# Half slabs, layer norm sums on ScalarE and an earlier first shift at the head of a gated long-convolution kernel

## The chip, the cores and the metric

The kernel runs on one core of a Trainium2 chip. The metric is the device time of one execution in microseconds (us); lower is better. The core's engines run side by side, each through its own list of instructions in order: TensorE (PE: matrix products and transposes, results in PSUM), VectorE (DVE), ScalarE (ACT), GpSimd (POOL) and SyncE (SP). SP, ACT and POOL also start DMAs. In the profile's rows L213 is line 213 of the kernel.

## What is computed

The forward pass normalises x, convolves a shifted and gated signal with a filter as long as the sequence, multiplies it by the output of a gated linear unit (silu on top), and adds x. The kernel returns this output and all gradients for a given grad_out.

```python
def forward(x, k, v, shift_k, ssm_k, ssm_D, w_gate, w_up, w_down):
    xn = (x - mean(x)) / sqrt(var(x) + 1e-5)           # over D = 1024
    k_shift = sum(k_pad[:, t:t + S] * shift_k[:, 3 - t] for t in range(4))
    kv = k_shift * v
    y = causal_conv(kv, ssm_k) + kv * ssm_D            # by rfft over 2 S
    s = xn * y
    h = (xn @ w_gate) * (xn @ w_up)                    # F = 3584
    return x + s * silu(h @ w_down)

out, vjp = jax.vjp(forward, ...)
return out, *vjp(grad_out)          # S = 2048, D = 1024, bfloat16
```

## The kernel before

S = 2048 rows are 16 row blocks of 128, F = 3584 columns are 14 slabs of 256 (`NSL`). The stages follow one another on TensorE, and the work of other engines is threaded between: first the gated unit's two input products, with the convolution's forward transform beside them (to about 546 us), then the down product, the backward products and the weight gradients.

**The head.** x comes in six chunks, `chunks = [(0, 1), (1, 1), (2, 2), (4, 4), (8, 4), (12, 4)]` (first block, number of blocks). SP loads them in program order between the weight slabs: x of chunks 0 and 1, slab 0 (up, then gate, 512 KB each), chunk 2, slab 1, chunks 3 to 5 (lines 866 to 872). `layer_norm` (line 554) does a chunk: for each block two `bn_stats` and a `bn_aggr` on VectorE give mean and variance, then a few small operations on all blocks of the chunk at once, with one square root on ScalarE (`root`), give 1/std (`RSTD`), and one `tensor_scalar` a block normalises it in place. TensorE turns each block, eight 128x128 transposes, and ScalarE copies it to `XNT`; the normalised rows are stored to `XNd` on POOL's queue. From block 8 on the turning is put off (`turn_rows`) and done by `turn_late` after the first group of the next unit.

**Units.** `gu_unit(sl, b0, n, w, tick)` (line 629) multiplies n blocks by one slab: n groups of eight products of 128x512 into one PSUM buffer `psg` (two of them), each emptied by a ScalarE cast into `gut`, which is stored to `GUd` on ACT's queue. VectorE multiplies the two halves to `hN`; POOL stores it to `Hd`, TensorE turns it five groups later, ScalarE copies it to `hT`, SP stores that to `HTd`. In the loop from line 881 the units of slabs 0 and 1 alternate with the layer norms; each layer norm is kept behind the last normalisation of the chunk before.

**The transform.** `conv_forward` (line 685) is a generator that yields the cost of each piece; `pump` runs it up to a fraction of the total, and `tick`, called once a group, sets that fraction: it grows in equal steps over `NT` ticks. The units in the loop have no tick (`nop`). The generator's first two steps load k and v (`load_kv`, on POOL's queue: four DMAs for k, four for v, 512-byte rows). Then come a filter load, `shift(0)` (four products with the taps `Wbc`, three sums, one product with v: eight VectorE operations on 128x4096), two turns of the filter, and eight rounds of Fourier transforms: TensorE products into `psF`, ScalarE copies to `SP`, long chains of VectorE sums `W`, `KX`, `HX`, and products back into `psY`. They need the sine tables `TF`: `mask_angles` on VectorE and `build_tables` on ScalarE (six functions and one table load), after the last layer norm.

**Order.** The program is traced in order and a scheduler orders each engine's list, earlier traced first among what is ready in its own model of time; this order is fixed before the kernel runs. `tc.issue_after(ins)` keeps the instructions of a block behind `ins` on the same engine, `keep_in_program_order` (`PIN`) keeps VectorE's transform in the traced order.

The lines in the head that set the order around the change, shortened:

```python
    if i == 3:                                  # line 894
        with tc.issue_after(xsts[4].ins):       # behind the store of chunk 4
            for _ in range(2):
                next(conv)                      # loads of k and v
    ...
    for i_, sl in ([(0, 0)], [(1, 0), (0, 1), (1, 1)], [(2, 0), (2, 1)],
                   [(3, 0), (3, 1)], [(4, 0)], [(5, 0)])[i]:
        gu_unit(sl, *xs[i_][0:2], slabs[sl], nop)
    ...
pump((SHIFT_W + 3.95) / F_TOTAL)                # line 925: shift(0)
for i_ in (4, 5):
    gu_unit(1, *xs[i_][0:2], slabs[1], tick)
```

Of the kernel before, what the change touches and what calls it, by code (L numbers as in the profile page):

```python
# [10 lines left out]
ACT = mybir.ActivationFunctionType  # L11
# [8 lines left out]
def build_kernel(  # L20
# [191 lines left out]
    def tt(o, a, b, op):  # L212
        pinned(V.tensor_tensor(o, a, b, op))  # L213
# [321 lines left out]

    def load_slab(sl, eng):
        w = fw.tile([P, DC, 2, SLW], BF16, name="wslab")
        fs = slice(sl * SLW, (sl + 1) * SLW)
        for a, wsrc in ((0, B_w_up), (1, B_w_gate)):
            last = eng.dma_start(out=w[:, :, a, :], in_=wsrc[:, fs].rearrange("(dc p) f -> p dc f", p=P))  # L540
        return w, last
# [9 lines left out]
    tr_ln, act_copy = [None], [None]  # L551
    turn_rows = []

    def layer_norm(b0, n, x4):
        def small(name, dt=F32):
            return lns.tile([P, 4], dt, name=name)[:, 0:n]
        mv = lns.tile([P, 4, 2], F32, name="mv")[:, 0:n, :]
        for i in range(n):
            bst = lns.tile([P, 2, 6], F32, name="bst")
            for hh in range(2):  # L560
                V.bn_stats(out=bst[:, hh, :], in_=x4[:, i, hh * 512:(hh + 1) * 512])
            V.bn_aggr(out=mv[:, i, :], in_=bst[:])
        var_b = small("var_b", BF16)
        V.tensor_copy(var_b, mv[:, :, 1])
        vpe = small("vpe", BF16)
# [11 lines left out]
        for i in range(n):  # L577
# [18 lines left out]
            for dc in range(DC):  # L596
                tr_ln[0] = nc.tensor.transpose(ps[:, dc, :], x4[:, i, dc * P:(dc + 1) * P], ident[:])
            act_copy[0] = nc.scalar.copy(out=XNT[q][:, :, qi * P:(qi + 1) * P], in_=ps[:])
        c, r0 = divmod(b0, 8)
        return last, root, st(xnn[:, c, r0:r0 + n, :], x4[:, 0:n, :])  # L600
# [84 lines left out]
    def conv_forward():  # L685
# [12 lines left out]
        def load_h(ds):  # L698
            hrow = U[5][:, 0:2048].rearrange("p (c u r) -> p c u r", c=2, r=8)
            cld(U[5][:, 0:2048], A_ssm_k[ds * P:(ds + 1) * P, :])  # L700
            S_["h", ds] = hrow

        def shift(dp):
# [9 lines left out]
            for j in (2, 1, 0):  # L713
                tt(prod, k[:, :, 3 - j:11 - j, :], wb(j), MUL)
                yield 2.3
                tt(acc, acc, prod, ADD)
                yield 2.3
# [42 lines left out]
        cf = pool("cf", 1)  # L760
        with tc.issue_after(xsts[3].ins):
            load_h(0)

# [89 lines left out]
        for _ in tl:  # L853
# [11 lines left out]
          for (b0, n) in chunks]  # L865
    for c in xs[0:2]:
        ln_load(*c)
    slabs = [load_slab(0, nc.sync)[0]]
    ln_load(*xs[2])
# [11 lines left out]
    for i, (b0, n, x4) in enumerate(xs):  # L881
# [9 lines left out]
        if i == 2:  # L891
            with tc.issue_after(xsts[-1].ins):
                spread_taps()
        if i == 3:
            with tc.issue_after(xsts[4].ins):
                for _ in range(2):
                    next(conv)
        if i == 4:
            with tc.issue_after(act_copy[0].ins):
                nc.scalar.activation(Dz[0:1, :], Dz[0:1, :], ACT.Copy, scale=WSC)  # L900
        for i_, sl in ([(0, 0)], [(1, 0), (0, 1), (1, 1)], [(2, 0), (2, 1)], [(3, 0), (3, 1)], [(4, 0)], [(5, 0)])[i]:
            gu_unit(sl, *xs[i_][0:2], slabs[sl], nop)
        if i == len(xs) - 1:
            with tc.issue_after(root.ins), tc.issue_after(last.ins):
                mask_angles(ang)
                build_tables(tg, ang)
    chunk[0] = len(xs)
    st(RSd.rearrange("(c u r) -> u c r", c=2, u=P), RSTD[:].rearrange("u (c r) -> u c r", c=2))
    st(RSTN[:], RSd.rearrange("(b p) -> p b", p=P))
    for p_ in (lnp, lns, tg, bsb):  # L910
        p_.release()
    ps_st.release()
    ps_cv = pool("ps_cv", 2, space=PSUM)
    pump, drain = make_pump(conv, F_TOTAL)
    cnt = [-5]
    NT = 24 * 8.0 + 17

# [6 lines left out]

    pump((SHIFT_W + 3.95) / F_TOTAL)
    for i_ in (4, 5):
        gu_unit(1, *xs[i_][0:2], slabs[1], tick)
# [708 lines left out]
```

## Time and profile before

| | us |
|---|---|
| time, median of 3 runs | 1929.6 (1929.02 to 1932.13) |
| the profiled execution, its own time | 1929.84 |
| its span, first to last instruction | 1928.1 |

| stretch, us | PE busy | DVE busy | ACT busy | POOL busy | DMA share |
|---|---|---|---|---|---|
| 0 to 10 | 7.06 | 6.98 | 2.96 | 6.04 | 0.80 |
| 10 to 20 | 8.82 | 7.70 | 4.43 | 3.34 | 1.07 |
| 20 to 50 | 27.71 | 27.48 | 20.72 | 17.03 | 0.86 |
| 50 to 73 | 23.00 | 20.12 | 19.98 | 5.00 | 0.90 |
| 73 to 367 | 293.47 | 290.79 | 170.26 | 54.73 | 0.71 |
| 367 to 488 | 118.02 | 119.86 | 67.28 | 14.34 | 0.73 |

The span is what lies between the first and the last instruction; the time of the execution holds 1.7 us more. Busy time is what an engine's instructions cover; starting a DMA is not counted. Where a row of the profile ends in square brackets, the engine stood idle for that long before it, and the name behind the arrow is what ended the wait. A line such as L213 is a helper (`tt`), so the tile names tell which step it is.

### The profile page before, as it was taken

The numbers are of one execution on the slowest core, as the hardware profiler recorded it, in microseconds if no ns is written. First come the engines' busy times: TensorE is split into PE (matmuls) and PEld (weight loads), VectorE is DVE, ScalarE is ACT, GpSimd is POOL, SyncE is SP. The second block draws the span as 40 slices with busy tenths as digits, with TensorE's granted clock in tenths as the row PEclk, the third lists the DMA queues.
The fourth block names the chain that finished last, engine by engine and source line by source line (L and its number), as shares of the span: only waits on it lengthen the run. The fifth ranks groups of instructions, "written<-read, shape, count | busy, mean of one in ns | idle before, by whom it ended". The sixth has DMA issues, their size and how long they took to land.

```text
span 1928.1 us, 27453 instructions
## 1 busy us (share of the span) xinstructions
PE 1914.2 (99%) x10978; PEld 1030.8 (53%) x10978; DVE 1542.1 (80%) x1695; ACT 638.8 (33%) x943; POOL 329.1 (17%) x461
## 2 busy tenths in 40 slices
PE   8999999999999999999999999999999999999999
PEld 5555655555444456665666666664444444444444
DVE  8999999999956555888799999999996403388884
ACT  5754655555332233343222222222222102011113
POOL 5121212201112210000122132021211101111111
PEclk9999999999999999999999999999999999999999
DMA  8776867659799988666788798585787999889984
GB/s 292 269 259 217 261 208 236 219 209 293 242 294 293 302 284 262 208 202 215 253 249 262 245 244 264 200 273 177 223 254 175 152 199 201 177 174 200 187 189 159
DMA packets 451360, 444.43 MB, mean 231 GB/s; under 512 B 268800, under 2 KB 371612, under 8 KB 436768
## 3 DMA queue, kind: packets, MB, share of 16 engines
q1 hardware_dynamic: 394848, 243.36, 47.7%
q0 software_dynamic: 40064, 169.95, 28.0%
q10 hardware_dynamic: 16320, 29.36, 4.1%
q8 instruction: 86, 1.41, 0.3%
q14 instruction: 42, 0.34, 0.1%
HBM read 194.00 MB, written 185.64 MB: 197 GB/s over the span
## 4 chain that ended last, share of the span: by engine, by line
PE 91%; DVE 6%; issue 1%; ACT 1%; DMA 0%; SPq 0%; ACTq 0%; DVEq 0%
PE psb L1344 20%; PE psx L1474 20%; PE psg L645 14%; PE psb L1327 10%; PE psbm L971 10%; PE psb L1422 9%; PE psF L235 3%; DVE W L213 2%; DVE HX L213 1%; PE tr L674 1%; PE psY L438 1%; DVE KX L213 1%; PE psY L1130 1%; PE psx L1422 1%; DVE U L213 1%
## 5 line engine op out<-in xcount | busy, mean ns | idle before, releaser
L645 PE MATMUL psg<-wslab,U 128*128 128x512 bf16 x1792 | 408.9, 380 | 3.4 <-DMA wslab<-in_B_w_gate_dram 2.5
L1344 PE MATMUL psb<-U,U 128*128 128x512 bf16 x1792 | 397.1, 379 | 0.0
L1474 PE MATMUL psx<-U,dgut 128*128 128x512 bf16 x1536 | 332.8, 379 | 0.0
L1474 PEld LDWEIGHTS <-dgut 128*128 128x128 bf16 x1792 | 175.1, 98 | 211.6
L1344 PEld LDWEIGHTS <-U 128*128 128x128 bf16 x1792 | 175.1, 98 | 198.1
L645 PEld LDWEIGHTS <-U 128*128 128x128 bf16 x1792 | 172.6, 98 | 189.0 <-issue 3.9
L1327 PE MATMUL psb<-wdt,U 128*128 128x256 bf16 x1792 | 205.6, 273 | 0.0
L1327 PEld LDWEIGHTS <-U 128*128 128x128 bf16 x1792 | 175.1, 98 | 29.4
L1422 PE MATMUL psb<-U,U 128*128 128x512 bf16 x816 | 177.1, 379 | 0.0
L213 DVE TENSOR_TENSOR W<-W 128x1024 f32<-128x1024 f32 (+1 forms) x174 | 171.5, 1002 | 3.7
L1349 ACT CAST wb<-psb 128x512 bf16<-128x512 f32 x112 | 65.6, 586 | 315.1 <-PE psb L1344 310.5
L971 PE MATMUL psbm<-U,ht 128*128 128x512 bf16 x672 | 145.7, 379 | 0.0
L1422 PEld LDWEIGHTS <-U 128*128 128x128 bf16 x896 | 87.4, 98 | 104.6
L647 ACT CAST gut<-psg 128x512 bf16<-128x512 f32 x156 | 91.4, 587 | 123.8 <-PE psg L645 123.4
L1506 ACT ACTIVATE dx_t<-dxn 128x1024 bf16<-128x1024 f32 x15 | 15.9, 1057 | 324.4 <-DVE dxn L213 324.4
L1182 DVE SCALAR_TENSOR_TENSOR dkp<-dkT,kT 128x1024 bf16<-128x1024 bf16 (+2 forms) x64 | 78.3, 1224 | 36.9 <-DMA dkT<-DKSHd 34.9
L971 PEld LDWEIGHTS <-ht 128*128 128x128 bf16 x672 | 65.5, 98 | 78.7
L213 DVE TENSOR_TENSOR U<-U,dht 128x2048 bf16<-128x2048 bf16 x56 | 68.3, 1220 | 45.7 <-ACT dht L1329 45.6
L1329 ACT CAST dht<-psb 128x512 bf16<-128x512 f32 x112 | 65.6, 587 | 116.4 <-PE psb L1327 116.4
L66 POOL DMA_DIRECT2D Hd<-hN x54 | 37.2, 688 | 296.3 <-DVE hN L213 294.1
L213 DVE TENSOR_TENSOR dxn<-psx,dxna_t 128x1024 f32<-128x1024 f32 x15 | 18.3, 1222 | 80.0 <-PE psx L1474 76.1
L1453 ACT CAST wbs<-psb 128x512 bf16<-128x512 f32 x51 | 29.9, 586 | 145.3 <-PE psb L1422 137.2
(237 smaller groups left out, 2451.5 us busy)
## 6 DMA issues: line engine op xcount, KB each, us to landing
U<-GUd SPq DMA_DIRECT2D x28, 1024.0 KB, 7.3
DGd<-U SPq DMA_DIRECT2D x28, 1024.0 KB, 6.4
GUd<-gut ACTq DMA_DIRECT2D x39, 512.0 KB, 6.1
out_dram<-wb SPq DMA_DIRECT2D x112, 128.0 KB, 4.3
U<-Hd SPq DMA_DIRECT2D x14, 1024.0 KB, 6.1
Hd<-hN POOLq DMA_DIRECT2D x54, 256.0 KB, 4.5
HTd<-hT SPq DMA_DIRECT2D x52, 256.0 KB, 3.7
ht<-HTd SPq DMA_DIRECT2D x6, 1536.0 KB, 9.7
```

Of the source, the lines that this page charges most:

```text
L213: pinned(V.tensor_tensor(o, a, b, op))
L235: mm = nc.tensor.matmul(ps[:, k].rearrange("p (c d) -> p c d", c=2), T[:, r, k, :], xr[:, r], start=(n == 0), stop=(n == len(rs) - 1 and ( ...
L645: gu_mm[0] = nc.tensor.matmul(ps[:], XNT[q][:, dc, qi * P:(qi + 1) * P], w[:, dc].rearrange("p a f -> p (a f)"), start=(dc == 0), stop=(dc ...
L647: nc.scalar.copy(out=gut[:, :, i], in_=ps[:].rearrange("p (a f) -> p a f", a=2))
L971: mm = nc.tensor.matmul(ps[:, dh * 512:(dh + 1) * 512], ht(fc)[:, i * P:(i + 1) * P], WD[fc // 4][:, fc % 4, dh * 512:(dh + 1) * 512], sta ...
L1182: ins = V.scalar_tensor_tensor(prod[:].rearrange("p r d -> p (r d)")[:, lo:H], dkT[:, 0, lo:H], 1.0, kT[:, 0, 13 + m + lo:13 + m + H], op0 ...
L1327: nc.tensor.matmul(ps[:, x * SLW:(x + 1) * SLW], DBMT[2 * hf + g][:, dc, (b % 4) * P:(b % 4 + 1) * P], wdt[:, dc, :], start=(dc == 0), sto ...
L1329: nc.scalar.copy(out=dht[:, 2 * e:2 * e + 2].rearrange("p b f -> p (b f)"), in_=ps[:])
L1344: nc.tensor.matmul(ps[:], XN[b // 4][:, b % 4, dc * P:(dc + 1) * P], dgus[b // 8][:, :, b % 8], start=(b == 0), stop=(b == NB - 1))
L1349: nc.scalar.copy(out=wb[:, dc % 2].rearrange("p a f -> p (a f)"), in_=ps[:])
L1422: nc.tensor.matmul(ps, h[:, f, b, :], DBM[b // 4][:, b % 4, dh * 512:(dh + 1) * 512], start=(b == 0), stop=(b == NB - 1))
L1474: nc.tensor.matmul(ps[:, dh * 512:(dh + 1) * 512], t[n][:, f, i * P:(i + 1) * P], WGU[n][:, f, dh * 512:(dh + 1) * 512], start=(n == 0 and ...
```

## The change

Five edits, all in the head.

- `load_slab` can load half of a slab (512 of the 1024 rows, up and gate, 256 KB each). Slab 0 is loaded in two halves, with chunk 1 of x between them, so that SP starts two DMAs more.
- In the chunks at blocks 4, 8 and 12 the last block's mean and variance are computed on ScalarE: the sum of the row by `Identity` with an accumulator, two small scalings, the sum of squared differences by `Square` with bias -mean, one small scaling. The first of these is kept behind an earlier ScalarE instruction (`hold`). `bn_stats` and `bn_aggr` remain for the other three blocks.
- The loads of k and v are traced one chunk earlier, behind the store of the chunk at block 4 and the broadcast of the taps; the first filter load has no hold any more.
- All products of `shift(0)` with the taps, and not only the first, are kept behind the last layer norm's last operation.
- The unit of slab 0 on blocks 12 to 15 moves out of the loop, behind the tables and behind the pump that traces `shift(0)`, and gets the tick; `NT` grows by 4.

```diff
@@ -533,9 +533,15 @@
     lns = pool("lns", 2)
     lnp = pool("lnp", 1)
 
-    def load_slab(sl, eng):
-        w = fw.tile([P, DC, 2, SLW], BF16, name="wslab")
+    def load_slab(sl, eng, part=None, w=None):
+        if w is None:
+            w = fw.tile([P, DC, 2, SLW], BF16, name="wslab")
         fs = slice(sl * SLW, (sl + 1) * SLW)
+        if part is not None:
+            cs_, rs_ = slice(4 * part, 4 * part + 4), slice(512 * part, 512 * part + 512)
+            for a, wsrc in ((0, B_w_up), (1, B_w_gate)):
+                last = eng.dma_start(out=w[:, cs_, a, :], in_=wsrc[rs_, fs].rearrange("(dc p) f -> p dc f", p=P))
+            return w, last
         for a, wsrc in ((0, B_w_up), (1, B_w_gate)):
             last = eng.dma_start(out=w[:, :, a, :], in_=wsrc[:, fs].rearrange("(dc p) f -> p dc f", p=P))
         return w, last
@@ -550,18 +556,30 @@
 
     tr_ln, act_copy = [None], [None]
     turn_rows = []
+    roots, copies = {}, {}
 
     def layer_norm(b0, n, x4):
         def small(name, dt=F32):
             return lns.tile([P, 4], dt, name=name)[:, 0:n]
         mv = lns.tile([P, 4, 2], F32, name="mv")[:, 0:n, :]
-        for i in range(n):
+        var_b = small("var_b", BF16)
+        own_ = n - {4: 1, 8: 1, 12: 1}.get(b0, 0)
+        hold = {4: act_copy[0], 8: roots.get(4), 12: copies.get(4)}.get(b0)
+        for i in range(own_, n):
+            junk = lnp.tile([P, D], BF16, name="junk")
+            s1, s2, negm = [lns.tile([P, 1], F32, name=nm_) for nm_ in ("s1", "s2", "negm")]
+            with tc.issue_after(hold.ins):
+                nc.scalar.activation(junk[:], x4[:, i, :], ACT.Identity, accum_out=s1[:])
+            nc.scalar.activation(negm[:], s1[:], ACT.Copy, scale=-1.0 / D)
+            nc.scalar.activation(mv[:, i, 0:1], s1[:], ACT.Copy, scale=1.0 / D)
+            nc.scalar.activation(junk[:], x4[:, i, :], ACT.Square, bias=negm[:], accum_out=s2[:])
+            nc.scalar.activation(var_b[:, i:i + 1], s2[:], ACT.Copy, scale=1.0 / D)
+        for i in range(own_):
             bst = lns.tile([P, 2, 6], F32, name="bst")
             for hh in range(2):
                 V.bn_stats(out=bst[:, hh, :], in_=x4[:, i, hh * 512:(hh + 1) * 512])
             V.bn_aggr(out=mv[:, i, :], in_=bst[:])
-        var_b = small("var_b", BF16)
-        V.tensor_copy(var_b, mv[:, :, 1])
+        V.tensor_copy(var_b[:, 0:own_], mv[:, 0:own_, 1])
         vpe = small("vpe", BF16)
         V.tensor_scalar(vpe, var_b, EPS, None, op0=ADD)
         half_r = small("half_r")
@@ -596,6 +614,7 @@
             for dc in range(DC):
                 tr_ln[0] = nc.tensor.transpose(ps[:, dc, :], x4[:, i, dc * P:(dc + 1) * P], ident[:])
             act_copy[0] = nc.scalar.copy(out=XNT[q][:, :, qi * P:(qi + 1) * P], in_=ps[:])
+        roots[b0], copies[b0] = root, act_copy[0]
         c, r0 = divmod(b0, 8)
         return last, root, st(xnn[:, c, r0:r0 + n, :], x4[:, 0:n, :])
 
@@ -711,7 +730,8 @@
                 tt(acc, k[:, :, 0:8, :], wb(3), MUL)
             yield 2.3
             for j in (2, 1, 0):
-                tt(prod, k[:, :, 3 - j:11 - j, :], wb(j), MUL)
+                with tc.issue_after(last.ins) if dp == 0 else nullcontext():
+                    tt(prod, k[:, :, 3 - j:11 - j, :], wb(j), MUL)
                 yield 2.3
                 tt(acc, acc, prod, ADD)
                 yield 2.3
@@ -758,8 +778,7 @@
         cx = pool("cx", 1)
         cs = pool("cs", 1)
         cf = pool("cf", 1)
-        with tc.issue_after(xsts[3].ins):
-            load_h(0)
+        load_h(0)
 
         def half(ds, x, i, first=None):
             if (ds, int(first is not None)) not in EIGHT:
@@ -863,9 +882,10 @@
     chunks = [(0, 1), (1, 1), (2, 2), (4, 4), (8, 4), (12, 4)]
     xs = [(b0, n, u8((4, 6, 7)[b0 // 4 - 1], a=4) if n == 4 else lnp.tile([P, n, D], BF16, name=f"x{b0}")[:])
           for (b0, n) in chunks]
-    for c in xs[0:2]:
-        ln_load(*c)
-    slabs = [load_slab(0, nc.sync)[0]]
+    ln_load(*xs[0])
+    slabs = [load_slab(0, nc.sync, 0)[0]]
+    ln_load(*xs[1])
+    load_slab(0, nc.sync, 1, slabs[0])
     ln_load(*xs[2])
     slabs.append(load_slab(1, nc.sync)[0])
     for c in xs[3:]:
@@ -891,29 +911,27 @@
         if i == 2:
             with tc.issue_after(xsts[-1].ins):
                 spread_taps()
-        if i == 3:
-            with tc.issue_after(xsts[4].ins):
                 for _ in range(2):
                     next(conv)
         if i == 4:
             with tc.issue_after(act_copy[0].ins):
                 nc.scalar.activation(Dz[0:1, :], Dz[0:1, :], ACT.Copy, scale=WSC)
-        for i_, sl in ([(0, 0)], [(1, 0), (0, 1), (1, 1)], [(2, 0), (2, 1)], [(3, 0), (3, 1)], [(4, 0)], [(5, 0)])[i]:
+        for i_, sl in ([(0, 0)], [(1, 0), (0, 1), (1, 1)], [(2, 0), (2, 1)], [(3, 0), (3, 1)], [(4, 0)], [])[i]:
             gu_unit(sl, *xs[i_][0:2], slabs[sl], nop)
-        if i == len(xs) - 1:
-            with tc.issue_after(root.ins), tc.issue_after(last.ins):
-                mask_angles(ang)
-                build_tables(tg, ang)
+    with tc.issue_after(root.ins), tc.issue_after(last.ins):
+        mask_angles(ang)
+        build_tables(tg, ang)
     chunk[0] = len(xs)
     st(RSd.rearrange("(c u r) -> u c r", c=2, u=P), RSTD[:].rearrange("u (c r) -> u c r", c=2))
     st(RSTN[:], RSd.rearrange("(b p) -> p b", p=P))
     for p_ in (lnp, lns, tg, bsb):
         p_.release()
+    turn_late()
     ps_st.release()
     ps_cv = pool("ps_cv", 2, space=PSUM)
     pump, drain = make_pump(conv, F_TOTAL)
     cnt = [-5]
-    NT = 24 * 8.0 + 17
+    NT = 24 * 8.0 + 21
 
     def tick(by=1):
         cnt[0] += by
@@ -923,6 +941,7 @@
             pump((SHIFT_W + (F_TOTAL - SHIFT_W) * (cnt[0] + 6.5) / (NT + 3.5)) / F_TOTAL)
 
     pump((SHIFT_W + 3.95) / F_TOTAL)
+    gu_unit(0, *xs[5][0:2], slabs[0], tick)
     for i_ in (4, 5):
         gu_unit(1, *xs[i_][0:2], slabs[1], tick)
     for sl in range(2, NSL - 2):
```

## The prediction

> **What bounds the kernel now.** I began with the page: TensorE is busy 1914.2 of 1928.1 us, so all that TensorE can ever get back is 13.9 us.
>
> ```profile
> PE 1914.2 (99%) x10978; PEld 1030.8 (53%) x10978; DVE 1542.1 (80%) x1695; ACT 638.8 (33%) x943; POOL 329.1 (17%) x461
> ...
> DVE  8999999999956555888799999999996403388884
> ACT  5754655555332233343222222222222102011113
> PEclk9999999999999999999999999999999999999999
> ```
>
> The second and third rows show where other engines come near their limit: VectorE (DVE) is at 9 tenths in slices 2 to 10 (48 to 482 us), and ScalarE (ACT) is at 7 in the slice from 48 us. The granted clock is full throughout, so it plays no part.
>
> Next, the waits of TensorE, longest first:
>
> ```profile
> PE tr L674 <- DVE hN L213: 3.0, 1, 3.0
> PE psg L645 <- DMA wslab<-in_B_w_gate_dram: 2.5, 2, 1.5
> PE tr L521 <- POOL ident masks.py:199: 1.4, 1, 1.4
> PE tr L597 <- DVE U L580: 1.0, 1, 1.0
> PE tr L606 <- DVE U L580: 0.7, 1, 0.7
> PE psg L645 <- ACT gut L647: 0.6, 1, 0.6
> PE psg L645 <- ACT U L587: 0.2, 1, 0.2
> ```
>
> They add up to 9.4 us (the rest is the store at the end, 3.6 us after the last matmul, and scraps). The change can reach all but the 1.4 us on `ident`. The timeline of TensorE places the ones that decide:
>
> ```profile
> 15.31 2.10 PE L645 MATMUL psg<-wslab,U 128*128 128x512 bf16 x9 [0.95 <-DMA wslab<-in_B_w_gate_dram]
> ...
> 26.30 1.99 PE L597 MATMUL tr<-ident,U 128*128 128x128 bf16 x32 [0.98 <-DVE U L580]
> ...
> 35.67 1.99 PE L606 MATMUL tr<-ident,U 128*128 128x128 bf16 x32 [0.72 <-DVE U L580]
> ...
> 40.63 3.61 PE L645 MATMUL psg<-wslab,U 128*128 128x512 bf16 x16 [0.59 <-ACT gut L647]
> ...
> 488.20 1.04 PE L674 MATMUL tr<-ident,hN 128*128 128x128 bf16 x8 [2.96 <-DVE hN L213]
> ```
>
> The last is the largest, and far from the edit. The chain of waits shows VectorE pieces without a break of TensorE from 368 to 488 us, ending in this `hN`. In the windows VectorE is busy 290.8 of 294 us (73 to 367) and 119.9 of 121 us (367 to 488): it runs behind TensorE's order the whole way, and at 488 the lag has eaten the buffers. What starts that run is in VectorE's timeline:
>
> ```profile
> 51.30 2.29 DVE L213 TENSOR_TENSOR U<-k,Wbc 128x4096 bf16<-128x4096 bf16 x1 [0.49 <-DMA k<-in_A_k_dram]
> ...
> 72.92 4.63 DVE L213 TENSOR_TENSOR W<-SP 128x1024 f32<-128x1024 f32 x4 [2.10 <-ACT SP L295]
> ```
>
> **The change, part by part.**
>
> *Slab halves: 0.* TensorE's first product now waits for the whole gate half of slab 0 (1.52 us, until 9.89). With halves, four of its eight matmuls can run earlier, but behind units (0,0) and (1,0) stands slab 1, which ends the wait at 15.31 (landed at 15.18). The bytes ahead of slab 1 are the same, and SP's issue of x2 already blocks for 2.45 us, which hides two more issues of 0.43 us. So what TensorE gains at 9.89 it waits at 15.31. x1 now stands behind 512 KB; at 261 to 332 GB/s (the page of this stretch) that is 1.5 to 2.0 us, from a landing at 5.2 (issue 1.66 plus 3.5) to about 7.0, against 6.89 at which VectorE asks for it; x2's 0.78 us of wait hides the 0.1. Bounds: -0.9 (all of the 0.95) to +0.5 (slab 1 later by an issue).
>
> *Three rows to ScalarE.* On VectorE a row costs two statistics and an aggregate, 1.15 + 0.11 = 1.26 us on the chain; three rows free 3.8 us. On ScalarE a row is five activations and two accumulator reads. `Square` and these forms are not in the trace; nearest are the sums of the last layer norm:
>
> ```profile
> 1708.41 1.06 ACT L1506 ACTIVATE dx_t<-dxn 128x1024 bf16<-128x1024 f32 x1 [63.60 <-DVE dxn L213]
> 1709.37 0.19 ACT L1506 ACTIVATION_READ_ACCUMULATOR dx_t<-dxn 128x1 f32 x1
> 1709.73 1.06 ACT L1508 ACTIVATE dx_t<-prod 128x1024 bf16<-128x1024 f32 x1 [0.17 <-DVE prod L213]
> ```
>
> Sum with read 1.15, gap 0.17, two small ones of 0.20 (the row of `half_r`), gap 0.17, square with read 1.15 (1.33 if the bias costs as in L1511, 1.24 us), gap 0.17, one of 0.20: 3.4; without gaps 2.9; I take 3.3, so 9.9 us for three, against ScalarE's idle 9.3 us in 20 to 50 us and 3.0 us in 50 to 73. That is tight, and it is the change's price.
>
> The Trainium skill, "ScalarE: Activation LUTs", section "Rules for kernel authors", says to put add- and multiply-like work on VectorE, faster per element there. The rows agree per row (1.26 against 3.3) and the rule speaks against the edit; by it alone the sum would be 6 us worse for three rows, but it counts neither engine's idle time.
>
> Chunk 4: its row may start when the copy before ends (20.34) and is done at 23.6, while VectorE ends its three rows at 18.91 + 3.78 = 22.7. Now the variance is complete at 24.24, so the chain gains 0.6 (0.98 if the row starts with no gaps; -0.4 if two casts of 0.59 go between). Value 0.6 of the 0.98 at 26.30. Chunk 8: VectorE saves 1.26 plus the 0.6 before; the 0.72 at 35.67 is gone (0 to 0.72). The 0.59 at 40.63 is four row copies of 0.94 in front of a cast; they come earlier, I take half, 0.3 (0 to 0.59).
>
> New stalls: with two accumulator buffers and 1.73 us per group, a cast of 0.59 may be 1.14 late. The longest piece on ScalarE, 1.06 + 0.19, is over that by 0.11; six such pieces, two hits: -0.2. Behind them on ScalarE stand casts, turned copies and GUd issues; TensorE waits for the casts. If a row runs unbroken it costs 3.3 + 0.59 - 1.73 = 2.2 of TensorE instead (first bound 0).
>
> *k's shift ahead of the last paceless unit.* Its loads move on POOL's queue from 37.80 to right behind the broadcast taps: four k issues (3.3 us) and four v issues (3.0 us) now stand ahead of two stores of normalised rows and several Hd stores, which nobody reads for hundreds of us; the Dz tile and `A_ssm_k` (no hold now; 4.4 us to land, needed at 64) lose nothing. k took 9 to 11 us to land, so it is there by about 42. VectorE's layer norms end at 46.5 - 3.8 = 42.7, masks 2.5 more: 45.2. Then the 1.09 and 0.49 us of gap before 51.30 go as well, and the shift ends some 5.4 us earlier (3.8 + 1.6), with part of the 2.10 at 72.92 as reserve if ScalarE has the six table functions (1.15 each) done; they are now emitted before the last unit's casts. The unit made paced puts the transform four groups (4 x 1.73 = 6.9 us) earlier in TensorE's order. NT grows by four, so at 488 the fraction of transform emitted is larger by about 0.0026 (187.5/216.5 against 183.5/212.5), 1.2 us of VectorE. Net lead there 4.2 to 6.3.
>
> To clear the stall VectorE must lead by 2.96 plus what TensorE gains before, 0.6 + 0.72 + 0.3 - 0.2 = 1.4: 4.4 in all, inside that lead. So 2.96 is taken whole (0 if the lead is under 1.4). What is late next: at 497 VectorE waits 3.34 for a cast, so the lag does not return; from there TensorE is never stopped till the end, and what is gained stays.
>
> **Sum** against the profiled execution (1929.84: span 1928.1 and 1.7 around it; the median 1929.6 is 0.24 lower, too little to matter): 1929.84 - 0.6 - 0.72 - 0.3 + 0.2 - 2.96 = 1925.5.
>
> **Rivals.**
> *A. ScalarE gives back what VectorE lends* (28%): casts are late by some 2 us in all between 20 and 60, the early waits stay in another name, only the lag wait goes: 1929.84 - 2.96 + 0.6 = 1927.5. For it: 9.9 us into 12.3 idle. Against: idle comes in pieces of 0.4 to 1.3 between casts, just where a piece fits.
> *B. ScalarE becomes the bound* (20%): at 20 to 36 us each row runs unbroken ahead of the casts, since it is emitted ahead of them, 3 x 2.2 = 6.6, and three of the tables in a row, 3.5 + 0.59 - 1.73 = 2.3; less 4.7 gained: 1929.84 + 8.9 - 4.7 = 1934.0. It decides once the casts are late by over 4.7 in all. That `Square` may not stand beside `Sqrt` in one table is the same rival: each of six reloads costs the 1.28 us of the page's table load, 7.7. Against: both tuned stretches have dependency gaps in which a cast can slip.
> *C. Slab 1 comes earlier too* (8%): the 0.95 at 15.31 and part of 1.0 at 26 and 40: 1925.5 - 0.95 - 0.6 = 1923.9. Against: same bytes, same queue.
> *D. The slab halves do nothing* is part of the forecast.
>
> **How the numbers follow.** The forecast has 44%, its own range 1924.5 to 1926.5 from the bounds above. About 0.2% (3.9 us) is what a measurement can tell from no change: 1925.7. Of the 44, 7 lie above it. Faster: 37 + 8 = 0.45; same: 7 + 28 = 0.35; slower 0.20. Range 1923.6 (C) to 1931.5: it holds the forecast, A and C and half the way to B.
>
> **What would show it.** Right: no wait of TensorE on `hN` near 480; layer norm of the last chunk done by 43; `U<-k,Wbc` starting near 45; first `W<-SP` at 66 to 69; the slab wait still ending near 15.2. Wrong: `psg <- ACT` in TensorE's waits above 1 us; a third table load before 50; VectorE waiting for `var_b` parts; the transform still starting near 72, which would leave the 2.96.

## The result and the profile after

The changed kernel takes **1932.39 us** (median of 20 runs, 1930.9 to 1936.66). In the same runs the kernel before took 1929.06 us (median of 20, 1927.31 to 1939.28). The ratio is 1.0016, with a 95% interval of 1.0009 to 1.0024, so the change costs some 3.3 us. The forecast was 1925.5 us, faster, and its range ended at 1931.5: the time is outside it, on the other side.

The profiled execution of the changed kernel took 1934.55 us, with a span of 1932.7 us (before: 1929.84 and 1928.1). From its page, busy times and the rows of 40 slices:

```profile
PE 1909.6 (99%) x10844; PEld 1033.1 (53%) x10978; DVE 1538.5 (80%) x1686; ACT 646.3 (33%) x964; POOL 329.9 (17%) x461
...
DVE  6999999999946555888799999999996403388884
ACT  6855555555522224333222222221222102011113
PEclk9999999999999999999999999999999999999999
```

TensorE's busy time looks smaller than before, but 134 of its 10978 matmul records are missing here, as the two counts beside PE and PEld show; it can't be compared. The row of ScalarE (ACT) shows 8 instead of 7 in the slice from 48 us: the engine that got the work is fuller exactly where it already stood highest. What can be compared are TensorE's waits. The list of what TensorE waited for, in us in total, times, longest:

```profile
PE psg L664 <- DMA wslab<-in_B_w_gate_dram: 3.0, 1, 3.0
PE tr L751 <- ACT hx L754: 1.6, 1, 1.6
...
PE psg L664 <- ACT gut_s L666: 1.3, 1, 1.3
PE psF L235 <- ACT hx L754: 1.3, 1, 1.3
PE psg L664 <- ACT U L666: 0.8, 1, 0.8
...
PE tr L693 <- DVE hN L213: 0.4, 1, 0.4
```

The wait on `hN` has fallen from 3.0 to 0.4 us, and the two on normalised rows, 1.0 and 0.7 us, are gone but for 0.2 (one of 0.6 us has come at the first chunks). In their place stand 3.0 us for the gate part of slab 1 (before: 1.52 us for slab 0 and 0.95 for slab 1, the 2.5 in two pieces of the list), and four entries on ScalarE of 0.8 to 1.6 us, where the kernel before has only 0.6 and 0.2. All listed waits add up to 11.7 us, against 9.4 before. The timeline of TensorE shows where they are:

```profile
16.91 4.00 PE L664 MATMUL psg<-wslab,U 128*128 128x512 bf16 x9 [3.04 <-DMA wslab<-in_B_w_gate_dram]
20.70 1.91 PE L615 MATMUL tr<-ident,x 128*128 128x128 bf16 x16
...
67.94 0.22 PE L751 MATMUL tr<-ident,U 128*128 128x128 bf16 x1 [1.64 <-ACT hx L754]
...
69.89 0.27 PE L235 MATMUL psF<-hx,TF 128*128 128x256 bf16 x1 [1.30 <-ACT hx L754]
...
494.18 0.62 PE L693 MATMUL tr<-ident,hN 128*128 128x128 bf16 x8 [0.43 <-DVE hN L213]
```

The nine products behind the slab take 4.00 us; before, the same nine took 2.10 us. The waits are not the whole price, and the windows of the same execution say why (columns: us, busy us and count of PE, PEld, DVE, ACT and POOL, then TensorE's granted clock, DMA share, GB/s):

```profile
12.00:15.00 3.00, 1.86 (x8) 0.66 (x8) 2.22 (x9) 1.58 (x4) 0.00 (x0) 1.00 1.08 398
15.00:18.00 3.00, 1.09 (x3) 0.44 (x4) 1.73 (x6) 0.00 (x0) 1.28 (x2) 0.68 1.04 422
18.00:21.00 3.00, 3.00 (x10) 1.21 (x9) 0.00 (x0) 0.48 (x1) 3.00 (x4) 0.50 1.01 413
21.00:24.00 3.00, 2.95 (x22) 2.14 (x21) 2.86 (x7) 2.03 (x3) 2.43 (x4) 0.68 1.00 407
...
68.00:72.00 4.00, 2.70 (x26) 2.35 (x26) 3.97 (x2) 4.00 (x6) 0.57 (x1) 0.84 0.42 117
72.00:76.00 4.00, 3.78 (x20) 2.28 (x20) 3.97 (x4) 2.78 (x4) 0.74 (x2) 0.74 0.56 231
```

The granted clock falls to 0.50 behind the slab wait and to 0.74 behind the waits near 68. In the profiled execution of the kernel before it is 1.00 in all these windows, and falls only once until the last product, from 488 to 492 us, behind the wait on `hN`:

```profile
488.00:492.00 4.00, 3.80 (x17) 1.98 (x18) 3.96 (x6) 1.50 (x2) 1.23 (x2) 0.57 1.07 413
```

So three things are to be told apart: the slab that lands later, the work that ScalarE can't take in time, and the clock. My theory after this reading was that each of the first two costs a part, since each has its own wait. The rivals: that one of them alone makes the whole loss; that the clock behind the slab wait does it; and that the gain at 488 never was worth what the forecast took.

### The profile page after: what moved, and what is told of

Its sections match the earlier page's. It is cut to its first block, busy times and chain, and to the rows that moved or that the text cites. A ratio compares the mean times of both kernels' runs of the same rounds, so it can differ in the third digit from the quotient of the medians.

```text
span 1932.7 us, 27330 instructions
## 1 busy us (share of the span) xinstructions
PE 1909.6 (99%) x10844; PEld 1033.1 (53%) x10978; DVE 1538.5 (80%) x1686; ACT 646.3 (33%) x964; POOL 329.9 (17%) x461
## 4 chain that ended last, share of the span: by engine, by line
PE 95%; ACT 2%; DVE 1%; issue 1%; DMA 1%; SPq 0%; ACTq 0%
PE psb L1363 20%; PE psx L1493 20%; PE psg L664 18%; PE psb L1346 10%; PE psbm L990 10%; PE psb L1441 9%; PE psF L235 3%; PE tr L693 1%; PE psY L438 1%; PE psY L449 1%; PE psY L1149 1%; PE psx L1441 1%; DMA wslab<-in_B_w_gate_dram 1%; DVE W L213 0%; PE tr L753 0%
## 5 line engine op out<-in xcount | busy, mean ns | idle before, releaser
L664 PE MATMUL psg<-wslab,U 128*128 128x512 bf16 x1734 | 403.8, 381 | 8.5 <-DMA wslab<-in_B_w_gate_dram 3.0
```

The lines of the kernel that those rows point to most:

```text
L664: gu_mm[0] = nc.tensor.matmul(ps[:], XNT[q][:, dc, qi * P:(qi + 1) * P], w[:, dc].rearrange("p a f -> p (a f)"), start=(dc == 0), stop=(dc ...
```

## The experiments

Each kernel below was timed against the kernel before on one chip (10 to 12 runs, the changed kernel 20; before's median was 1929.06 in the run of the result, 1929.14 in the series of e1, e4, e5 and e6, 1929.09 in that of e7, e8, e10 and e11, and 1929.52 in that of e3, e12 and e13). Much of the spread within a kernel goes with TensorE's clock: the shortest run of each has a mean granted clock of 1.000, and those at 0.998 are some 1.5 to 8 us longer (not all: two of the changed kernel's, 1933.13 and 1936.14 us, have 1.000). Of each kernel one execution was profiled.

| kernel | median us | lowest to highest | ratio to before, 95% interval |
|---|---|---|---|
| after | 1932.39 | 1930.9 to 1936.66 | 1.0016 (1.0009 to 1.0024) |
| e1 after, filter held | 1930.19 | 1929.97 to 1933.04 | 1.0003 (0.9995 to 1.0011) |
| e3 the same, no ScalarE rows | 1928.60 | 1926.88 to 1936.91 | 1.0002 (0.9991 to 1.0012) |
| e4 before, filter free | 1931.04 | 1928.63 to 1934.27 | 1.0007 (0.9998 to 1.0016) |
| e5 before, slab halves | 1929.35 | 1927.87 to 1930.14 | 0.9998 (0.9990 to 1.0007) |
| e6 before, ScalarE rows | 1929.81 | 1927.95 to 1932.23 | 1.0001 (0.9993 to 1.0009) |
| e7 before, shift ahead | 1929.07 | 1926.94 to 1934.63 | 1.0000 (0.9989 to 1.0010) |
| e8 after, filler in the slab wait | 1933.63 | 1931.57 to 1937.22 | 1.0021 (1.0011 to 1.0031) |
| e10 before, NT 19 | 1925.30 | 1924.81 to 1931.06 | 0.9981 (0.9971 to 0.9990) |
| e11 e1 with before's pace | 1934.25 | 1931.45 to 1936.43 | 1.0022 (1.0013 to 1.0031) |
| e12 before, NT 21 | 1925.98 | 1924.24 to 1931.03 | 0.9981 (0.9972 to 0.9991) |
| e13 e10 with one ScalarE row | 1926.30 | 1925.02 to 1938.83 | 0.9991 (0.9977 to 1.0005) |

And what the profiled executions show, the waits being the sum of each list of TensorE's waits:

| kernel | span | waits | of them before 80 us | span less waits | mean clock |
|---|---|---|---|---|---|
| before | 1928.1 | 9.4 | 6.4 | 1918.7 | 0.999 |
| after | 1932.7 | 11.7 | 10.9 | 1921.0 | 0.997 |
| e1 | 1928.6 | 11.3 | 10.5 | 1917.3 | 1.000 |
| e3 | 1925.1 | 9.0 | 8.6 | 1916.1 | 1.000 |
| e4 | 1932.5 | 12.1 | 7.4 | 1920.4 | 0.998 |
| e5 | 1927.8 | 10.2 | 7.0 | 1917.6 | 0.999 |
| e6 | 1926.2 | 9.2 | 6.0 | 1917.0 | 1.000 |
| e7 | 1925.2 | 9.2 | 8.4 | 1916.0 | 1.000 |
| e8 | 1931.2 | 10.5 | 9.7 | 1920.7 | 0.999 |
| e10 | 1923.9 | 7.0 | 5.4 | 1916.9 | 1.000 |
| e11 | 1930.8 | 12.0 | 8.8 | 1918.8 | 0.999 |
| e12 | 1924.2 | 8.2 | 6.3 | 1916.0 | 1.000 |
| e13 | 1923.2 | 6.6 | 6.0 | 1916.6 | 1.000 |

Where the clock is 1.000, the span less the waits is 1916.0 to 1917.3 us whatever the kernel. What lies above that I take for slow clock (in e8 also for its filler). By this table the changed kernel's span is longer by 2.3 us of waits and by 2.3 us of slow clock. That holds for these two executions and not for the medians: the changed kernel's was 2.2 us above its median, e4's was the longest of its kernel, and those of e3, e6, e7 and e13 were the shortest of theirs.

**e1 and e4: the filter load.** In the changed kernel `load_h(0)` has no hold. e1 gives it back, and e4 takes it away from the kernel before and does nothing else:

```diff
# e1, against the changed kernel (e4: the reverse, against the kernel before)
-        load_h(0)
+        with tc.issue_after(xsts[3].ins):
+            load_h(0)
```

> The changed kernel with the first filter load held again behind the store of the chunk at block 4. Theory Q (the 512 KB filter load, now started at 7.85 us on POOL's queue, takes DMA bandwidth from slab 1): slab 1 lands near 15.2 to 15.5 instead of 16.9, TensorE's wait on it falls from 3.0 to 1.5 or less, the granted clock stays at 1.00 in 15 to 24 us, and the time falls by 2 to 5 us against the changed kernel. Theory H (the halves and their two extra issues delay slab 1): the wait stays at 2.5 to 3.0 and the clock at 0.5 to 0.7. Theory R (the ScalarE rows set the time) expects VectorE's waits for var_b of 2.8 and 3.3 us to stay, and no more than 1 us of gain.

> The kernel before with one edit: the first filter load has no hold. Theory Q: the load goes out near 8 us, slab 1 lands 1.3 to 1.7 us later than 15.2, the wait on it grows from 0.95 to about 2.5, and the time rises by 1.5 us if the clock holds and by 3 to 5 us if it drops. Theories H and R: no change of the wait, time within 0.5 us of the kernel before.

e1 took 1930.19 us, 2.2 us less than the changed kernel; eleven of its twelve runs are below the fastest of the changed kernel's twenty. e4 took 1931.04, 1.9 us more than before. POOL's timeline in the changed kernel shows the load that is let go:

```profile
7.85 0.54 POOL L66 DMA_DIRECT2D U<-in_A_ssm_k_dram  x1
```

It starts at 7.85 us; in the kernel before it starts at 34.30. The 512 KB go out while slab 1 (issued at 4.88 and 5.37) is still under way, and TensorE gets its gate part at 16.9 us instead of 15.3 (in the other profiled executions with the filter held, at 14.3 to 15.4). TensorE's timeline of e4, with that edit alone:

```profile
17.20 3.71 PE L645 MATMUL psg<-wslab,U 128*128 128x512 bf16 x9 [3.62 <-DMA wslab<-in_B_w_gate_dram]
```

It has the same wait and the same slow products as the changed kernel. In e1 the wait is 1.57 us and the nine products take 2.10:

```profile
15.39 2.10 PE L664 MATMUL psg<-wslab,U 128*128 128x512 bf16 x9 [1.57 <-DMA wslab<-in_B_w_gate_dram]
```

So the freed load costs about 2 us in the medians, by itself and with the rest; that the slab lands later for it is shown in both directions, while the interval of e4's ratio, 0.9998 to 1.0016, just reaches 1.

**e5: the slab halves.**

```diff
-    for c in xs[0:2]:
-        ln_load(*c)
-    slabs = [load_slab(0, nc.sync)[0]]
+    ln_load(*xs[0])
+    slabs = [load_slab(0, nc.sync, 0)[0]]
+    ln_load(*xs[1])
+    load_slab(0, nc.sync, 1, slabs[0])
```

> The kernel before with slab 0 in two halves alone. Theory H: slab 1 lands 1 us or more later and the time rises by 1 to 3 us. Theory Q: slab 1 lands within 0.3 us of 15.2, the first wait (1.52 us at 9.89) shrinks and the wait at 15.3 grows by as much, and the time is within 1 us of the kernel before.

1929.35 us against 1929.14: nothing that can be told from zero, and its runs are the steadiest of all. The wait on slab 0 shrinks from 1.52 to 0.79 us, but two of 0.9 us on the first normalised rows come, and the products of slab 1 start at 15.44 us, as before (15.31): the halves are off the path, behind slab 1.

**e6: the three ScalarE rows alone.** The kernel before with the new `layer_norm`.

```diff
+        own_ = n - {4: 1, 8: 1, 12: 1}.get(b0, 0)
+        for i in range(own_, n):
...
+                nc.scalar.activation(junk[:], x4[:, i, :], ACT.Identity, accum_out=s1[:])
```

> The kernel before with the three ScalarE rows alone (slab 0 whole, loads, filter hold, shift and paced unit as before). Theory R: VectorE waits 2 to 6 us in all for variances from ScalarE, the layer norm of the last chunk ends later than 46.5, the transform starts later than 72.9, and the time rises by 1 to 4 us. The prediction's own step: the last layer norm ends 2.5 to 4 us earlier and the time falls by 1 to 3 us.

1929.81 us: nothing again. TensorE's two waits on the layer norm are gone from its list, and waits on ScalarE's casts (`gut_s` 1.3, `U` 0.8, `gut` 0.4 us, where the kernel before has 0.6 on `gut`) have come: they cancel. VectorE was lent 3.8 us and gave them back: it waits 1.11, 0.39 and 3.70 us for `var_b`, and the first product of the transform, `W<-SP`, starts at 72.95 us (before: 72.92).

**e7: the shift ahead alone.** The kernel before with the early loads of k and v, the held products, unit (5,0) paced behind the shift, and `NT` 21. No rows on ScalarE, slab 0 whole, the filter held.

```diff
# against the changed kernel; the hunk that loads slab 0 whole again is left out
-        own_ = n - {4: 1, 8: 1, 12: 1}.get(b0, 0)
+        own_ = n - {}.get(b0, 0)
...
-        load_h(0)
+        with tc.issue_after(xsts[3].ins):
+            load_h(0)
```

> The kernel before with the fourth and fifth edits and the early loads of k and v alone (slab 0 whole, no ScalarE rows, first filter load held). Theory M (the part moves the wait: the transform now stands in TensorE's order before ScalarE has the tables and the turned filter): the 3.0 us wait on hN near 488 goes, TensorE waits 2.5 to 5 us on ScalarE between 56 and 76 instead, and the time is within 1.5 us of the kernel before. The prediction's own step: no new wait, the layer norms at their old time, time lower by 2 to 4 us. Theory R' (the waits in 56 to 76 come only from the ScalarE rows making ScalarE late): no such waits here, time lower by 3 us.

1929.07 us, no change, though the wait on `hN` is gone (0.4 us) and the transform starts 5 us earlier on VectorE, as its timeline shows:

```profile
67.86 4.62 DVE L213 TENSOR_TENSOR W<-SP 128x1024 f32<-128x1024 f32 x4
```

The timeline of TensorE near 60:

```profile
61.21 0.22 PE L751 MATMUL tr<-ident,U 128*128 128x128 bf16 x1 [0.51 <-ACT hx L754]
...
63.16 0.27 PE L235 MATMUL psF<-hx,TF 128*128 128x256 bf16 x1 [1.29 <-ACT hx L754]
```

With unit (5,0) behind the shift, the first transposes and the first products of the transform follow each other before ScalarE has done the tables and the turned copies of the filter, and TensorE waits for `hx`, which it did nowhere in the kernel before. In this execution, its shortest (1926.94 us), all of TensorE's waits add up to 9.2 us against 9.4: the gain at 488 is nearly all exchanged. Half of its twelve runs are above 1929.5, at clocks of 0.999 and 0.998; what slowed them isn't shown.

**e3: after without the rows, filter held.** Against e1 it takes out only the rows, with the shift ahead in both:

```diff
-        own_ = n - {4: 1, 8: 1, 12: 1}.get(b0, 0)
+        own_ = n - {}.get(b0, 0)
```

> The changed kernel with the first filter load held and all layer norm statistics on VectorE: the same as e1_filter_held but for the three ScalarE rows. Theory R (with the shift ahead, the rows make ScalarE late for tables, casts and turned filter): VectorE's waits for variances (5.3 us in all) go, TensorE's waits on ScalarE between 24 and 76 (6 us in e1) fall by 3 us or more, the best third of the runs lies 2 to 3 us below that of e1. Theory N (rows neither cost nor gain): same time as e1 within 0.7 us.

1928.60 us, against 1930.19 in e1 (another series, whose kernel before was 0.4 us faster). The intervals of the two ratios overlap, because four of e3's runs are long (1930.53 to 1936.91 us, two of them at a clock of 0.998). But eight of its twelve runs are below the fastest of e1, and the shortest four lie 2.3 to 3.1 us below the shortest four of e1, as theory R had it; TensorE's waits on ScalarE between 24 and 76 us fall from 5.5 to 2.4 us. So the same rows that cost nothing alone cost about 1.6 us in the median (2 with the series' offset) where the shift is ahead. The normalisation of the last chunk starts at 47.66 us in e1 and at 44.00 in e3, and `W<-SP` at 71.40 and 67.96: the 3.7 us arrive at the transform nearly whole (3.4; some 0.5 of it is slab 1, which came later in e1's execution). In e6 a like delay was hidden in VectorE's own waits: in front of the shift they are 1.09 and 0.49 us before and none in e6, in front of `W<-SP` 2.10 before and 1.47 in e6. e1 and e3 have none of these left. How the row comes to delay it, VectorE's timeline of the changed kernel shows, where it is longest:

```profile
28.56 0.17 DVE L584 TENSOR_SCALAR vpe<-var_b 128x4 bf16<-128x4 bf16 x1 [2.81 <-ACT var_b L576]
...
49.40 0.40 DVE L584 TENSOR_SCALAR vpe<-var_b 128x4 bf16<-128x4 bf16 x1 [3.32 <-ACT var_b L576]
...
58.69 2.28 DVE L213 TENSOR_TENSOR U<-k,Wbc 128x4096 bf16<-128x4096 bf16 x1
...
75.44 3.49 DVE L213 TENSOR_TENSOR W<-SP 128x1024 f32<-128x1024 f32 x3
```

and ScalarE's timeline of the same execution has the reason:

```profile
38.10 1.06 ACT L572 ACTIVATE junk<-U 128x1024 bf16<-128x1024 bf16 x1
39.06 0.20 ACT L572 ACTIVATION_READ_ACCUMULATOR junk<-U 128x1 f32 x1
...
40.23 3.76 ACT L626 COPY U<-tr 128x1024 bf16<-128x1024 bf16 x4
...
46.94 1.15 ACT L575 ACTIVATE junk<-U,negm 128x1024 bf16<-128x1024 bf16 x1
...
49.15 0.22 ACT L576 ACTIVATE var_b<-s 128x1 bf16<-128x1 f32 x1
59.26 1.28 ACT L181 ACT_TABLE_LOAD   x1
...
66.88 1.00 ACT L754 ACTIVATE hx<-tr 128x1024 bf16<-128x1024 bf16 x1
67.79 1.14 ACT L184 ACTIVATE TF<-ab__918,mhpi 128x1024 bf16<-128x1024 f32 x1
68.83 1.00 ACT L754 ACTIVATE hx<-tr 128x1024 bf16<-128x1024 bf16 x1
```

The row's first half is done at 39.3 us. Then four row copies, 3.76 us in all, four casts, two turned copies and a wait of 0.96 us for TensorE come in the engine's fixed order, and `Square` starts at 46.94. The row itself is some 3 us of work, yet 11.3 us pass from its start at 38.10 to its variance at 49.4, while VectorE, which would have needed 1.26 us, stands idle for 3.32.

**e11: before's pace on top of e1.** The rival here was that the paced unit itself pulls the transform forward too far, so that starting it four groups later would end the waits on `hx`.

```diff
-    cnt = [-5]
-    NT = 24 * 8.0 + 21
+    cnt = [-9]
+    NT = 24 * 8.0 + 17
```

> The changed kernel with the first filter load held and the transform's start in TensorE's order put back by four groups (count from -9, NT 17 again); shift of k still ahead of the last unit of slab 0. Theory M: the waits on the turned filter and on kv between 60 and 76 go or fall under 1 us, the 3 us wait near 488 comes back unless VectorE's first transform sum starts before 70; time between -2 and +1 us of the kernel before. Theory R': waits on ScalarE in 56 to 76 stay at 3 us or more, since ScalarE is late for its rows' sake.

1934.25 us, the slowest of all. The list of TensorE's waits in e11:

```profile
PE tr L693 <- DVE hN L213: 3.0, 1, 3.0
...
PE tr L693 <- ACT hx L754: 1.3, 1, 1.3
...
PE tr L751 <- ACT hx L754: 1.1, 1, 1.1
```

Half of the theory held: with before's pace and start the wait on `hN` is back at 3.0 us (`W<-SP` starts at 73.63). The other half fell: the waits on `hx` stay at 1.3 and 1.1 us. The count moves the first products of the transform (from 65.84 to 70.98 us), but not the turns of the filter in front of them, which stand with the shift (63.89 us in e1, 63.38 here) and wait for ScalarE all the same. Whether turns put later would end these waits isn't shown.

**e10 and e12: the pace alone.** If the pace decides at 488, it needs nothing else of the change. The kernel before, one number changed (19 in e10, 21 in e12):

```diff
-    NT = 24 * 8.0 + 17
+    NT = 24 * 8.0 + 19
```

> The kernel before with one number changed: NT 17 to 19, so that the transform is spread over two more ticks. Theory L (VectorE's lag alone makes the 3.0 us wait at 488, and with it a stretch at a lower clock): at that point 0.8% of 460 us, 3.7 us, less VectorE work stands ahead, the wait goes, and the time falls by 2 to 4.5 us below the kernel before. Rival: the work left over delays the transform's end and returns as a wait of TensorE or VectorE after 520: same time within 1 us.

> The kernel before with NT 21 in place of 17: twice the step of e10_slower_pace, the same number as in the changed kernel but with the transform's start where it was. Theory L: the 3.0 us wait is already gone at 19, so 21 gives the same as 19 within 0.7 us; the rival (left-over transform work comes back after 520) gives 1 to 4 us more than 19.

1925.30 and 1925.98 us, both 0.9981 of before (intervals up to 0.9990 and 0.9991). These beat both kernels. The timeline of TensorE in e10 at the place of the old wait:

```profile
486.73 0.62 PE L674 MATMUL tr<-ident,hN 128*128 128x128 bf16 x8 [0.60 <-DVE hN L213]
487.19 3.40 PE L645 MATMUL psg<-wslab,U 128*128 128x512 bf16 x15
```

2.96 us of wait have become 0.60, and the products after it run at full clock; in e12 no wait on `hN` is left, but a wait on a cast (`gut`, 1.9 us) has come. Between the two nothing can be told. The gain in the median, 3.8 us, is more than the 2.4 us of wait: the kernel before can also lose time to the clock behind it (17 products in 5.04 us). The shortest runs of the two, both at a clock of 1.000, differ by 2.3 us (1924.81 against 1927.13), as much as the wait alone.

**e13: one row that might pay.** e10 with the ScalarE row in the chunk at block 8 alone, where the wait for the variance was smallest (0.39 us).

```diff
# the one line in which its layer_norm differs from the changed kernel's
-        own_ = n - {4: 1, 8: 1, 12: 1}.get(b0, 0)
+        own_ = n - {8: 1}.get(b0, 0)
```

> The kernel before with NT 19 and a ScalarE row in the chunk at block 8 alone, where VectorE waited least for it (0.39 us). If a row pays wherever ScalarE is free in time: the wait of 0.72 us at 35.67 goes and the time is 0.3 to 0.8 us below e10_slower_pace. If a row costs ScalarE more than it frees on VectorE even there: 0.5 to 1.5 us above it.

1926.30 us, ratio 0.9991 (0.9977 to 1.0005) against 0.9981 in e10: no gain can be shown, a loss can't either. VectorE waits 1.51 us for that variance now, where it waited 0.39 with the two other rows on ScalarE as well: a wait read in one kernel's order doesn't hold in another's.

**e8: the clock.** The changed kernel, with 40 small products of the warm-up kind behind unit (1,0), so that TensorE has something to do while slab 1 lands.

```diff
+        if i == 1:
+            gu_unit(0, *xs[1][0:2], slabs[0], nop)
+            with tc.issue_after(gu_mm[0].ins):
+                keep_busy(40)
... (the same unit is taken out of the loop's list)
```

> The changed kernel with 40 small products on a spare PSUM tile (2.2 us of TensorE work whose result nobody reads) put into TensorE's wait for slab 1, which stays as long. Theory C (after some 3 us idle TensorE runs at half the clock for 4 to 6 us): the granted clock stays at 1.00 in 15 to 24, TensorE's nine products at 17 take 2.1 instead of 4.0 us, and the median time falls by 1 to 3 us against the changed kernel. Theory W (only the idle time itself costs): same time as the changed kernel within 0.5 us.

The clock stays at 1.00 from 12 to 27 us, as that expectation's theory C had it, but the time doesn't fall: 1933.63 us against 1932.39 (the intervals of the two ratios overlap). TensorE's timeline of e8:

```profile
14.32 1.89 PE L521 MATMUL tr<-ident 128*128 128x128 bf16 x31
16.64 1.07 PE L615 MATMUL tr<-ident,x 128*128 128x128 bf16 x16 [0.42 <-DVE x L598]
17.55 0.67 PE L521 MATMUL tr<-ident 128*128 128x128 bf16 x9
18.06 5.56 PE L664 MATMUL psg<-wslab,U 128*128 128x512 bf16 x23
```

The filler (rows of L521) is 2.56 us of TensorE's own time, and its tail stands in front of the slab's products, which start at 18.06 us, later than the 16.91 of the changed kernel. The waits between 60 and 70 us stay (1.64 and 1.30 us on `hx`), with the clock at 0.57 from 68 to 72 us. So the slow clock behind the slab is real, but whether removing it alone would bring time is not shown by this run: the filler also changed the order of what follows (VectorE now waits only 0.64 and 0.19 us for variances).

## Why the prediction failed

**What held.** The halves at 0 (e5). VectorE's lag is where the wait on `hN` comes from: less transform ahead of that point (e10, e12) takes it away, and nothing is late again behind it. No table load was added: `Square` runs beside `Sqrt`, and the first load that follows is at 59.26 us, for the sines.

**Right by luck: the wait on `hN`.** It goes in the changed kernel, as forecast, but not by the forecast lead. The first `W<-SP`, to come "at 66 to 69", starts at 75.44, 2.5 us later than before, and a start "near 72" was to leave the wait. VectorE starts the `hN` in question (its 50th in either execution) at 493.44 us, 6.0 us later than before (487.46); only, TensorE gets there 8.5 us later (it stands ready at 493.75, against 485.24). The wait is covered by the loss in the head.

**The failed step: the filter load.** "the Dz tile and `A_ssm_k` (no hold now; 4.4 us to land, needed at 64) lose nothing". True of the load itself, false of its neighbour. I asked who waits for the moved transfer and not whose bytes it joins, though the same prediction argued from bytes for the slab halves: slab 1 "the bytes ahead of slab 1 are the same". They were, but 512 KB more now moved beside them. Cost in the medians: 2.2 us (e1), 1.9 us alone (e4).

**The failed step: when ScalarE can do the rows.** The size of a row was right (taken at 3.3 us, between 2.9 and 3.4; 3.19 us of busy time measured in the first, 3.66 from its start to its variance with two casts between). The order was wrong, least for the first: "its row may start when the copy before ends (20.34) and is done at 23.6". It started at 20.79 in e1 and was done at 24.5 (24.86 and 28.5 in the changed kernel, behind the late slab). For the third no chain was followed, and that row took 11.3 us: "VectorE's layer norms end at 46.5 - 3.8 = 42.7" became 53.6 in the changed kernel and 49.6 in e1. I subtracted three rows of VectorE without adding the chain through ScalarE: the layer norm waits for the later of the two. Alone that is hidden (e6), with the shift ahead it costs (e1 against e3).

**Mis-sized: the late casts.** Two late casts were put at 0.2 us in the sum. In e6 they are 1.3 (`gut_s`) and 0.8 us (`U`), in the changed kernel the same, in e1 1.3 and 1.3: more than the 1.6 us that the rows were to gain in front of TensorE. This is what rival A had, casts "late by some 2 us".

**The failed step: four groups earlier for free.** "The unit made paced puts the transform four groups (4 x 1.73 = 6.9 us) earlier in TensorE's order" is right: its first product starts at 63.16 us in e7, at 70.27 before. But the sum has no cost for it. VectorE gets the reserve in front of `W<-SP`; TensorE pays, which now comes to the filter's turns before ScalarE has the tables: it waits 1.8 us for `hx` in e7, 2.4 in e1 and 2.9 in the changed kernel. The condition "if ScalarE has the six table functions (1.15 each) done" was written down and not worked out; ScalarE's queue from 59 to 70 us in the changed kernel has the table load, six table functions, two turned copies of the filter and four casts, with no gap in which anything else could go.

**Mis-sized: the lead at 488.** The forecast let VectorE lead by 4.2 to 6.3 us there: 5.4 from the rows and the gaps, less "1.2 us of VectorE" for the larger fraction, with a reserve of 2.10. e7 has no rows and starts `W<-SP` 5.1 us earlier than before (the 2.10 and the gaps are gone, and one `hN` less stands between), yet starts that 50th `hN` only 1.8 us earlier (485.69 against 487.46). On the way VectorE stands idle for 2.8 us, against 0.6 before (1.86 us of it at 241.69, for a cast): started earlier, it catches up with TensorE's order and gives a part of the lead back. What is left of the 2.96 goes because TensorE itself comes 0.8 us later. e10 and e12 get at the same wait from the other side: with two or four steps more in `NT` and nothing else, less transform stands ahead of that point, and 2.4 us of the wait or all of it go. The earlier start, with what it costs, was not needed for the prize.

**Mis-sized: the prize, and the clock.** "The granted clock is full throughout, so it plays no part" was read from 40 slices of 48 us. In windows of 4 us the kernel before has a stretch at 0.57 behind the very wait that the forecast was about, so clearing it could be worth more than the wait: in e10's execution the waits are 2.4 us less and the span less waits another 1.8. In the same way new waits cost more than their length.

**The sum again**, each median against that of the kernel before in its own series: shift and halves without rows and with the filter held, -0.9 us (e3); with the rows, +1.1 (e1), so that the rows add 2.0; with the filter load freed as well, +3.3 (the changed kernel), so that it adds 2.3. Neither -0.9 nor +1.1 can be told from 0 by its interval. By the shortest run of each kernel the steps are -0.4, +2.7 and +3.6: there the rows add 3.1 and the filter load 0.9. So both cost time, and which costs more depends on the runs compared. The forecast had -4.4. Of the rivals B came nearest in number, 1934.0 us for ScalarE as the bound; but it put 8.9 us on late casts, which are 2.1 us here, and neither it nor another rival had the variances, the turned filter or the slab. Three slips in the working change nothing: VectorE is at 9 tenths in slices 2 to 11 (to 530 us), the fractions of the transform differ by 0.0025, and the gains that rival B subtracts add up to 4.6.

## What to carry to other kernels

When a load is let go earlier, ask whose bytes it joins, not only who waits for it: the transfer it delays may be the one that the matrix engine is waiting for. Work moved to an engine with idle time is worth what the fixed order of that engine leaves it: follow the moved chain piece by piece between the neighbours it gets, and take the later of the two chains. And before moving work to clear a lag, try the number that sets the pace: here one constant gave 3.8 us, where five edits together made a loss.

## What the runs showed of the chip

I had not expected a TensorE wait of 3 us to cost up to another 2.7 us behind it (from the start of the nine products behind the slab wait to that of the 30 behind the next turn, it is 5.50 us in the changed kernel, 16.91 to 22.41, and 2.84 in e1, 15.39 to 18.23). In windows of 1 us the clock is granted at half for some 3.5 us after it (488 to 491.5 in the kernel before) and once for 7 (16 to 23 in the changed kernel), but not always: e6 has the same wait on `hN` as the kernel before, in the same place, and no slow stretch. TensorE's timeline of e6:

```profile
487.90 0.62 PE L693 MATMUL tr<-ident,hN 128*128 128x128 bf16 x8 [2.96 <-DVE hN L213]
488.36 3.83 PE L664 MATMUL psg<-wslab,U 128*128 128x512 bf16 x17
```

Seventeen products in 3.83 us, against 5.04 in the profiled execution of the kernel before. Of the five profiled executions with this wait of 2.96 to 3.05 us between 487 and 492 (before, e4, e5, e6, e11), e6 alone kept the full clock. The Trainium skill, "TensorE: Matmul & The Clock Gate", section "Part 1: The HAM clock gate (the "warmup" mystery)", says that the gate drops to half rate after an idle window of about 3.4 us, and that the window runs freely, so that the moment of a change depends on where in it the products fall. The rows agree with the half rate (0.50 granted in the windows that lie wholly in such a stretch) and with the chance in it; that waits of 2.96 and 3.04 us can already suffice, below the stated window, is what these executions show. Waits of 1.64 and 1.30 us close together were followed by it too (at 0.74 in the changed kernel, at 0.57 in e8), and in e1 and e11, with 1.15 and 1.29, they were not.
